# Filter units of four residue classes instead of 128 neighbouring frequencies in a spectral FFN kernel on one Trainium2 core

## The chip, the cores and the metric

The kernel runs on one core of one Trainium2 chip. The metric is device microseconds of one execution; each time is the median of several executions. The engines are PE (matrix multiplies; PEld is its weight load), DVE (vector), ACT (scalar and activation), POOL and SP; POOL and SP also issue DMAs.

## The reference

```python
def _A_ref(x, w_r, w_i):                      # x [1, 2048, 1024], w [2048, 513]
    X = jnp.fft.rfft2(x, axes=(-2, -1))
    X = X * (w_r + 1j * w_i)
    return jnp.fft.irfft2(X, s=(2048, 1024), axes=(-2, -1))
def _B_ref(x, w1, w2):                        # w1 [1024, 3584], w2 [3584, 1024]
    return jnp.einsum("bsf,fd->bsd", _silu(jnp.einsum("bsd,df->bsf", x, w1)), w2)
xn = _layernorm(x)
return x + _A_ref(xn, w_r, w_i) * _silu(_B_ref(xn, w1, w2))
```

All inputs are float32. Two chains start from the layer norm: a feed-forward net (two large products) and a filter in the frequency domain. They meet in the last line.

## The kernel before, in words

**Products.** Each float32 factor is split into two float16 halves (high on ACT, low on DVE), and a product is three float16 matmuls of 128x512. The first product, `mm1`, makes 112 tiles `pa` (4 column groups c of the sequence by 28 feature blocks f) of 24 matmuls each. A tile lies in one of four PSUM buffers (tag `ff`) until ACT takes it out with a SiLU (L441). Four such tiles become `h32`, whose halves `hosum` and `hoone` (L228, L231) are stored by seven DMAs (L464). The second product, `mm2`, is written as seven products m = 0 to 6 of half size over eight row tiles j: 56 tiles `pb` of 42 matmuls each (L510 to L512). The weights of each m are split in 14 steps; a step waits for its raw block `jr`, loaded by POOL (L388).

**The filter.** It runs beside the products, in stages that share PE, DVE and ACT with them:

- Forward: `fa_mat` (L742) transforms rows; ACT takes the result out of PSUM into `L0` (L751, L752), after a DVE memset of one column (L750). `fd_gen` does butterflies on DVE into the tile `V`, then a step R of radix 4 per frequency group j; the halves `Rs` (ACT, L819) are stored to `vd[j]` (POOL, L823).
- `wmax_gen`: the largest filter weight, needed for scaling; 18 loads of 128x912 by SP and 18 reductions on DVE (L859), without stores.
- `f_gen`: 16 filter units u = 4q + j, each 128 rows of the sequence frequency (residue q) by the 128 neighbouring row frequencies of group j. A unit loads `vq` and weights `wq`, runs the matmuls `fx` (L912 to L914) into one of two PSUM buffers (tag `ft`), copies half of it (`xc`, ACT, L935), makes X (DVE), scales the weights by `zs` (ACT, L994), multiplies, makes Z (DVE), and splits Z into halves `zq` (`high_z` on ACT, L952; `low_z` on DVE, L957). Each split is five pieces, since `zq` is ordered by residue class of the row frequency (modulo 16) while a unit holds neighbours. `zq` has one buffer per q; four DMAs (L962) store it when the fourth unit of q is done.
- `edge_gen`: the last frequency column, from `xsv`, 32 small loads by POOL (L1027).
- `i_gen`, for c in the order 1, 3, 0, 2: loads `zt` from `zd[c]` (L1119), runs `iu` (L1146) in four pieces; each is copied by ACT (`uw`, L1153), worked on by DVE, split again (`us`, ACT, L1175); then matmuls `id` (L1188), a copy `sw` (L1195) and butterflies on DVE.

**What sets the order.** Every engine works through its list in order. The lists are written by one Python loop over the `pa` tiles and then the `pb` tiles. After each tile, `work()` takes a step from `wq` (weights), three times in four a step from `xq` (the maxima, the edge), and as many steps from `bg` (the FFT stages) as a cost model of PE and DVE finds room for: a `clock` to which `meter` adds a cost for each instruction as it is written. So fewer or cheaper DVE instructions bring later steps forward in all lists. `defer(n, ...)` issues a store n ticks later; `stores[0]` is SP at first and POOL from the end of the layer norm.

```python
            clock["dve"] = max(clock["dve"], clock["pe"] - 1.0)
            for _ in range(3):
                if clock["dve"] > clock["pe"] + LEAD or hold[0] or slot(bg) == PAUSE:
                    break
```

Tile pools hand out buffers by tag; an instruction that writes a buffer waits for whoever still reads what was in it, stores included.

Of the kernel before, what the change touches and what calls it, by code (L numbers as in the profile page):

```python
# [44 lines left out]
def make_constants():  # L45
# [8 lines left out]
    ca[:, :, 64] = np.where(d0[:, :, 0] % 2 == 0, 1.0, -1.0)  # L54
    ca = np.stack(_halves(ca, 2.0**14), 1)
# [49 lines left out]
def spectral_ffn(ctx, tc, x, w_r, w_i, w1, w2, ca, kc, ci, tw, pm, out):  # L105
# [20 lines left out]
    zd = [dp.tile([128, 4, 2, 1024], F16, name=f"zd{c}") for c in range(4)]  # L126
# [16 lines left out]
    turn2 = cp.tile([128, 128], F32, name="turn2")  # L143
# [459 lines left out]
    A = {}  # L603
# [143 lines left out]
    def fa_evac(c, p):  # L747
        ps = psa.pop((c, p))
        t0 = A["p"].tile([128, 8, 2, 65], F32, name=f"L0_{c}_{p}", tag="L0", bufs=2)
        nc.vector.memset(t0[:, :, 1, 0:1], 0.0)  # L750
        nc.scalar.activation(t0[:, :, 0], ps[:, :, 0:65], AF.Copy)  # L751
        nc.scalar.activation(t0[:, :, 1, 1:64], ps[:, :, 65:128], AF.Copy)  # L752
        l0[c, p] = t0

    def fd_gen(c):
        ap = A["p"]
        vt = ap.tile([128, 4, 2, 512], F32, name=f"V{c}", tag="V", bufs=1)

        def bfly(p):
# [4 lines left out]
            e = ap.tile([128, 4, 2, 65], F32, name=f"E{c}_{p}", tag="E", bufs=1)  # L764
# [3 lines left out]
            ee = ap.tile([128, 2, 2, 65], F32, name=f"EE{c}_{p}", tag="EE", bufs=1)  # L768
            eo = ap.tile([128, 2, 2, 65], F32, name=f"EO{c}_{p}", tag="EO", bufs=1)
# [4 lines left out]
            pq = ap.tile([128, 2, 4, 65], F32, name=f"PQ{c}_{p}", tag="PQ", bufs=1)  # L774
# [16 lines left out]
            tt(v[:, :, 0:65], ee[:, 0], ee[:, 1], op=OP.add)
# [12 lines left out]
            tt(v[:, 1, 0:1], ee[:, 0, 0, 0:1], ee[:, 1, 0, 0:1], op=OP.subtract)  # L804
# [20 lines left out]
        for j in range(4):  # L825
            sl = slice(128 * j, 128 * j + 128)
            if j:
                high_r(j - 1)
# [19 lines left out]
    def wmax_gen():  # L848

        ap = A["p"]  # L850
        mt = small("mw", 18)
        tl = {}
        for k in range(21):
            if k < 18:
                src = (w_r, w_i)[k % 2].rearrange("(p r) k -> p (r k)", p=128)
                tl[k] = ap.tile([128, 912], F32, name=f"wm{k}", tag="x", bufs=4)
                nc.sync.dma_start(tl[k], src[:, 912 * (k // 2):912 * (k // 2) + 912])
            if k >= 3:
                nc.vector.tensor_reduce(mt[:, k - 3:k - 2], tl.pop(k - 3), axis=AX.X, op=OP.max, apply_absolute_value=True)  # L859
# [21 lines left out]
    def f_gen():  # L881
# [36 lines left out]
        for n, t_ in enumerate((ones, ident, turn2)):  # L918
            nc.gpsimd.dma_start(t_, pm[:, n])
# [17 lines left out]
        def by_class(u):  # L937

            j = u % 4
            zv = zs_[u].rearrange("m n (i l) -> m n l i", l=16)  # L940
            qv = [zqs[u // 4][:, k].rearrange("m (n l) i -> m n l i", l=16)[:, :, :, 8 * j:8 * j + 8] for k in range(2)]
            for first, n, to, by in ((1, 3, 0, 4), (4, 4, 14, -4), (9, 4, 3, 4), (13, 3, 9, -4)):
                stop = to + by * (n - 1) + (1 if by > 0 else -1)
                yield zv[:, :, first:first + n], [v[:, :, to:stop if stop >= 0 else None:by] for v in qv]
            yield zv[:, :, 0:9:8], [v[:, :, 12:14] for v in qv]

        def high_z(u):
            q, j = u // 4, u % 4
            if j == 0:
                zqs[q] = bp.tile([128, 2, 128, 32], F16, name=f"zq{q}", tag="zq", bufs=1)  # L950
            for z, o in by_class(u):
                nc.scalar.activation(o[0], z, AF.Copy)  # L952

        def low_z(u):
            q, j = u // 4, u % 4
            for z, o in by_class(u):
                nc.vector.tensor_tensor(o[1], z, o[0], op=OP.subtract)  # L957
# [10 lines left out]
        for u in range(16):  # L968
# [24 lines left out]
            for w in (wr, wi):  # L993
                nc.scalar.activation(w, w, AF.Copy, scale=zs)  # L994
# [34 lines left out]
    def edge_gen():  # L1029
# [267 lines left out]
    with tc.manual_schedule():  # L1297
# [79 lines left out]
        for n, (c, f) in enumerate(order):  # L1377
# [20 lines left out]
            if 44 <= n < 76:  # L1398
                load_edge(n - 44)
# [107 lines left out]
```

## Time and profile before

| what | value |
|---|---|
| median of 3 executions | 1247.46 us (1245.87 to 1251.45) |
| the profiled execution's own time | 1247.57 us |
| its span in the trace | 1245.8 us |
| DMA moved | 296.88 MB, mean 238 GB/s |
| HBM read, written | 186.97 MB, 104.33 MB |

The span runs from the first to the last instruction in the trace. Busy shares are means over stages with different limits, so a change in a stage is judged by that stage's own rows. In a row of a group, "x" is the count; behind the first bar stand the busy time and the mean in ns of one; behind the second the idle time of the engine just ahead of these instructions and what ended it. In a row of the timeline the first number is the start and the second the duration, and the brackets hold the idle time ahead and its releaser.

### The profile page before, as it was taken

To read this page: it belongs to the slowest core of one execution; us is meant where nothing else is said; L and a number is where in the kernel's file an instruction comes from. 1 tells how busy PE (TensorE), PEld (TensorE's weight loads), DVE (VectorE), ACT (ScalarE), POOL (GpSimd) and SP (SyncE) were. 2 spreads that over 40 slices of the span, in tenths; PEclk is the share of its full clock that TensorE was granted. 3 is DMA by queue.
4 is the path that set the end of the run, shared out by engine and by line. 5 is a ranking of instruction groups with operands and counts; after the bars stand their busy time and mean duration, and the time that the engine had idled before them with its cause. 6 is when DMAs were issued, how large, how long until landed. Compare 5 with 4: busy or idle time off the path is not lost. (4 is left out here: it accounts for less than half of the span.)

```text
span 1245.8 us, 20664 instructions
## 1 busy us (share of the span) xinstructions
PE 1225.4 (98%) x7759; PEld 621.0 (50%) x7759; DVE 1018.9 (82%) x2056; ACT 499.4 (40%) x672; POOL 321.1 (26%) x526
## 2 busy tenths in 40 slices
PE   8999999999999999999999999999999998999997
PEld 5545454445455444445545555554555544545544
DVE  6678999998988998565958799894895886895985
ACT  4765354344256356443534335232222222322211
POOL 1341231232444545342333021204123030010000
PEclk9999999999999999999999999999999999999999
DMA  7477475665577789766887889959779699696688
GB/s 239 124 184 192 126 247 171 192 189 159 156 237 229 236 282 332 254 228 180 196 274 229 264 250 245 295 146 360 234 216 301 207 322 375 248 330 240 231 297 317
DMA packets 161733, 296.88 MB, mean 238 GB/s; under 512 B 32048, under 2 KB 84912, under 8 KB 161120
## 3 DMA queue, kind: packets, MB, share of 16 engines
q1 hardware_dynamic: 125392, 183.49, 47.8%
q0 software_dynamic: 36096, 111.93, 28.6%
q8 instruction: 61, 1.00, 0.3%
q14 instruction: 40, 0.33, 0.1%
q10 hardware_dynamic: 144, 0.13, 0.0%
HBM read 186.97 MB, written 104.33 MB: 234 GB/s over the span
## 5 line engine op out<-in xcount | busy, mean ns | idle before, releaser
L432 PE MATMUL pa<-xnT,w 128*128 128x512 f16 x2688 | 585.1, 379 | 2.6 <-DVE xnT L686 1.7
L432 PEld LDWEIGHTS <-w 128*128 128x128 f16 x2688 | 262.3, 98 | 313.4 <-issue 2.0
L510 PE MATMUL pb<-w,ht 128*128 128x512 f16 (+1 forms) x798 | 300.3, 376 | 0.4 <-DMA ht<-hd_one 0.4
L511 PE MATMUL pb<-w,ht 128*128 128x512 f16 (+1 forms) x798 | 300.0, 376 | 0.0
L512 PE MATMUL pb<-w,ht 128*128 128x512 f16 (+1 forms) x798 | 300.0, 376 | 0.0
L512 PEld LDWEIGHTS <-ht 128*128 128x128 f16 x798 | 78.2, 98 | 91.5 <-issue 0.8
L510 PEld LDWEIGHTS <-ht 128*128 128x128 f16 x798 | 78.3, 98 | 90.3 <-issue 0.8
L511 PEld LDWEIGHTS <-ht 128*128 128x128 f16 x798 | 78.3, 98 | 87.2 <-issue 0.6
L441 ACT ACTIVATE h<-pa,s 128x512 f32<-128x512 f32 x112 | 75.2, 677 | 76.7 <-PE pa L432 70.0
L231 DVE SCALAR_TENSOR_TENSOR w<-jr,sc,w 128x512 f16<-128x512 f32 x98 | 71.9, 745 | 33.9 <-ACT w L228 33.8
L228 ACT ACTIVATE w<-jr,sc 128x512 f16<-128x512 f32 x98 | 68.6, 714 | 76.7 <-DMA jr<-in_B_w_dram 69.6
L388 POOL DMA_DIRECT2D jr<-in_B_w_dram x56 | 36.7, 655 | 226.0 <-issue 162.1
L464 POOL DMA_DIRECT2D hd_sum<-hosum x52 | 38.2, 771 | 183.1 <-DVE hosum L231 116.7
L228 ACT ACTIVATE hosum<-hr,hs 128x1536 f16<-128x1536 f32 x28 | 44.0, 1573 | 88.7 <-DVE hr L471 48.0
L952 ACT ACTIVATE zq<-Z 128x192 f16<-128x192 f32 (+2 forms) x80 | 37.2, 542 | 104.0 <-DVE Z L218 67.4
L228 ACT ACTIVATE hoone<-h,hs 128x2048 f16<-128x2048 f32 x28 | 56.0, 1998 | 53.3 <-DMA hd_one<-hoone 22.7
L231 DVE SCALAR_TENSOR_TENSOR hoone<-h,hs,hoone 128x2048 f16<-128x2048 f32 x28 | 65.6, 2343 | 12.0 <-ACT hoone L228 12.0
L470 DVE TENSOR_TENSOR hr<-h 128x1024 f32<-128x1024 f32 x28 | 34.2, 1220 | 35.3 <-ACT h L441 35.1
L464 POOL DMA_DIRECT2D hd_one<-hoone x52 | 46.0, 884 | 66.1 <-DVE hoone L231 21.1
L231 DVE SCALAR_TENSOR_TENSOR hosum<-hr,hs,hosum 128x1536 f16<-128x1536 f32 x28 | 50.7, 1811 | 3.2 <-ACT hosum L228 3.2
L228 ACT ACTIVATE w<-w1r,rs 128x1024 f16<-128x1024 f32 x28 | 31.8, 1143 | 47.6 <-DVE w L231 26.4
L591 ACT ACTIVATE pl<-pl,c 128x512 f32<-128x512 f32 (+1 forms) x26 | 17.0, 683 | 74.7 <-DVE pl L570 45.6
(215 smaller groups left out, 1798.4 us busy)
## 6 DMA issues: line engine op xcount, KB each, us to landing
jr<-in_B_w_dram POOLq DMA_DIRECT2D x84, 256.0 KB, 7.3
w1r<-in_B_w_dram SPq DMA_DIRECT2D x28, 512.0 KB, 5.9
w2m<-in_B_w_dram SPq DMA_DIRECT2D x28, 512.0 KB, 6.3
ht<-hd_dif SPq DMA_DIRECT2D x32, 448.0 KB, 9.5
ht<-hd_sum SPq DMA_DIRECT2D x32, 448.0 KB, 6.2
ht<-hd_one SPq DMA_DIRECT2D x32, 448.0 KB, 7.0
hd_sum<-hosum POOLq DMA_DIRECT2D x52, 256.0 KB, 4.5
hd_one<-hoone POOLq DMA_DIRECT2D x52, 256.0 KB, 4.5
```

Of the source, the lines that this page charges most:

```text
L228: nc.scalar.activation(hi, raw, AF.Copy, scale=scale)
L231: nc.vector.scalar_tensor_tensor(lo, raw, scale, hi, op0=OP.mult, op1=OP.subtract)
L388: nc.gpsimd.dma_start(raw[n], ws[m][q] if m in ws else w2_block(m, q, 0))
L432: nc.tensor.matmul(ps, w[:, wh, d], xt[:, xh, d], start=(n == 0), stop=(n == 23))
L441: nc.scalar.activation(hq[:, 2 * (c % 2) + f % 2], ps, AF.Silu, scale=s1[:, f:f + 1])
L464: defer(1, lambda k=k, m=m: stores[0].dma_start(hd[m, g][:, :, q].rearrange("f p h s -> f p (h s)"), o[:, k].rearrange("f p h s -> f p (h ...
L470: tt(sums[:, 0:2], hq[:, 0::2], hq[:, 1::2], op=OP.subtract)
L510: nc.tensor.matmul(ps, hh[:, 0], w[:, 0], start=first, stop=False)
L511: nc.tensor.matmul(ps, hh[:, 0], w[:, 1], start=False, stop=False)
L512: nc.tensor.matmul(ps, hh[:, 1], w[:, 0], start=False, stop=last)
L591: nc.scalar.activation(o, o, AF.Silu, scale=c2)
L952: nc.scalar.activation(o[0], z, AF.Copy)
```

## The change

The columns of the forward matrix `ca` are put in another order, so that the 128 frequencies of a filter unit are four residue classes of 32 instead of 128 neighbours.

- `fd_gen`: `V` becomes [128, 4, 2, 17, 32], and butterflies write runs of four elements; rows are 68 wide instead of 65, filled by two memsets on POOL instead of one on DVE; two ACT copies per c are new; R goes through j = 3, 2, 1, 0, and for j > 0 its sums and differences take two instructions instead of one (14 instead of 8 per c).
- `wmax_gen`: 16 steps of two loads of 128x512; the last column's maximum comes from `xsv`, in a new job `wmax_end`. Each step also copies its tile in the new column order by five ACT copies into `wc`, which shares the four buffers of tag `x` with the loads, and stores `wc` by two DMAs of 256 KB to the new DRAM tiles `wp`: 80 ACT copies and 32 stores.
- `f_gen` reads the weights from `wp`. The scaling of `wq` goes; `zs` is applied in the splits of Z, which are one instruction per unit (two for j = 0). `zq` is a buffer of its own per unit, two in turn. `zd` is one DRAM tile; each unit stores 512 KB in runs of 256 bytes, where a store before had runs of 2 KB. Three constants are loaded at u = 4 instead of ahead of the stage.
- `load_i` has two DMAs; the loads of `xsv` stand 20 tiles earlier.

```diff
     ca[:, :, 64] = np.where(d0[:, :, 0] % 2 == 0, 1.0, -1.0)
+    col = np.arange(64)
+    kk = 16 * (col % 4) + col // 4
+    ca = ca[:, :, np.concatenate([kk, 64 + kk])]
...
-    zd = [dp.tile([128, 4, 2, 1024], F16, name=f"zd{c}") for c in range(4)]
+    zd = dp.tile([128, 4, 16, 4, 128], F16, name="zd")
+    wp = [dp.tile([S, 512], F32, name=f"wp{i}") for i in range(2)]
...
-        t0 = A["p"].tile([128, 8, 2, 65], F32, name=f"L0_{c}_{p}", tag="L0", bufs=2)
-        nc.vector.memset(t0[:, :, 1, 0:1], 0.0)
-        nc.scalar.activation(t0[:, :, 0], ps[:, :, 0:65], AF.Copy)
+        t0 = A["p"].tile([128, 8, 2, 68], F32, name=f"L0_{c}_{p}", tag="L0", bufs=2)
+        nc.gpsimd.memset(t0[:, :, 1, 0:1], 0.0)
+        nc.gpsimd.memset(t0[:, :, :, 65:68], 0.0)
+        nc.scalar.activation(t0[:, :, 0, 0:65], ps[:, :, 0:65], AF.Copy)
...
-        for j in range(4):
-            sl = slice(128 * j, 128 * j + 128)
...
-            nc.vector.tensor_tensor(b, vt[:, 0:2, :, sl], vt[:, 2:4, :, sl], op=OP.add)
-            nc.vector.tensor_tensor(d, vt[:, 0:2, :, sl], vt[:, 2:4, :, sl], op=OP.subtract)
...
+        for j in (3, 2, 1, 0):
+            parts = ((0, 12, 4),) if j == 0 else ((4 - j, 12 + j, 8 + 2 * j), (4 + j, 12 - j, 8 - 2 * j))
...
+            for o_, op in ((b, OP.add), (d, OP.subtract)):
+                ov = o_.rearrange("a p r (n l i) -> a n (p r) l i", n=len(parts), i=32)
+                for n, (la, lz, st) in enumerate(parts):
+                    nc.vector.tensor_tensor(ov[:, n], *(rows_[:, k:k + 4, la:lz + 1:st] for k in (0, 4)), op=op)
...
-                tl[k] = ap.tile([128, 912], F32, name=f"wm{k}", tag="x", bufs=4)
-                nc.sync.dma_start(tl[k], src[:, 912 * (k // 2):912 * (k // 2) + 912])
...
+                tl[k] = ap.tile([128, 2, 512], F32, name=f"wm{k}", tag="x", bufs=4)
+                for i in range(2):
+                    nc.sync.dma_start(tl[k][:, i], (w_r, w_i)[i][128 * k:128 * k + 128, 0:512])
+            if k >= 2:
+                t_, o = tl.pop(k - 2), ap.tile([128, 2, 512], F32, name=f"wc{k}", tag="x", bufs=4)
+                nc.vector.tensor_reduce(mt[:, k - 2:k - 1], t_, axis=AX.XY, op=OP.max, apply_absolute_value=True)
...
+                nc.scalar.activation(o.rearrange("m r (l i) -> m r l i", i=32)[:, :, 0:4], src[:, :, 0:13:4], AF.Copy)
+                for n, (la, st) in enumerate(((3, -1), (13, 1), (5, 1), (11, -1))):
+                    nc.scalar.activation(dst[:, :, n, 1:4], src[:, :, la:la + 3 * st:st], AF.Copy)
+                for i in range(2):
+                    defer(1, lambda o=o, i=i, k=k: stores[0].dma_start(wp[i][128 * k - 256:128 * k - 128, :], o[:, i]))
...
-            if j == 0:
-                zqs[q] = bp.tile([128, 2, 128, 32], F16, name=f"zq{q}", tag="zq", bufs=1)
+            zqs[u] = bp.tile([128, 2, 8, 128], F16, name=f"zq{u}", tag="zq", bufs=2)
             for z, o in by_class(u):
-                nc.scalar.activation(o[0], z, AF.Copy)
+                nc.scalar.activation(o[0], z, AF.Copy, scale=zs)
...
-            for w in (wr, wi):
-                nc.scalar.activation(w, w, AF.Copy, scale=zs)
...
-            if j == 3:
-                zv = zqs[q].rearrange("m h (c n) i -> m h c (n i)", c=4)
-                for c in range(4):
-                    defer(1, lambda c=c: stores[0].dma_start(zd[c][:, q], zv[:, :, c]))
+            defer(1, lambda: stores[0].dma_start(
+                zd[:, q, :, 3 - j], t_.rearrange("m h n k -> m (h n) k")))
...
-            if 44 <= n < 76:
-                load_edge(n - 44)
+            if 24 <= n < 56:
+                load_edge(n - 24)
```

What this does to the order shows at three places. In these rows the first entry is the line (in the changed kernel lines stand a few later), then the operation, what it writes and reads with a running number behind each name, and the size.

First ACT in the forward stage, between the `pa` tiles of f = 6 and 7. `hosum`, `hoone` and `w1` are the splits of the hidden values and weights. Before:

```order
L751 ACTIVATE L0_1_0_1935<-fa1_0_1885 128x8x65 [waits PE_49]
L752 ACTIVATE L0_1_0_1935<-fa1_0_1885 128x8x63
L441 ACTIVATE h32_3_0_1785<-pa1_7_1850,s1_224 128x512
L228 ACTIVATE w1_9_1970<-w1r9_1567,rs1_223 128x1024 [waits DMAHW2_49,DVE_49,Activation_49]
L751 ACTIVATE L0_1_1_2000<-fa1_1_1910 128x8x65 [waits PE_49]
L752 ACTIVATE L0_1_1_2000<-fa1_1_1910 128x8x63
L228 ACTIVATE hosum_0_3_0_2043<-hr3_0_1965,hs_226 128x12x128 [waits DMASW7_49,DMASW1_49,DMASW0_49]
L441 ACTIVATE h32_3_1_2046<-pa2_6_1939,s1_224 128x512 [waits PE_49]
```

and now:

```order
L445 ACTIVATE h32_3_0_1799<-pa1_7_1880,s1_222 128x512 [waits PE_49]
L232 ACTIVATE w1_9_1950<-w1r9_1570,rs1_221 128x1024 [waits DMAHW2_49,DVE_49,Activation_49]
L877 ACTIVATE wc4_1955<-wm2_1801 128x2x128 [waits DMAHW1_49,DMAHW2_49,DMASW1_49,DMASW0_49]
L879 ACTIVATE wc4_1955<-wm2_1801 128x2x3x32 x4
L756 ACTIVATE L0_1_0_2013<-fa1_0_1963 128x8x65 [waits PE_49,Pool_49]
L757 ACTIVATE L0_1_0_2013<-fa1_0_1963 128x8x63
L232 ACTIVATE hosum_0_3_0_2044<-hr3_0_1945,hs_224 128x12x128 [waits DMASW6_49,DMASW5_49,DMASW4_49]
L445 ACTIVATE h32_3_1_2047<-pa2_6_1919,s1_222 128x512
L877 ACTIVATE wc5_2057<-wm3_1857 128x2x128 [waits DMAHW3_49,DMASW3_49,DMAHW4_49,DMASW2_49,Activation_49]
L879 ACTIVATE wc5_2057<-wm3_1857 128x2x3x32 x4
L756 ACTIVATE L0_1_1_2089<-fa1_1_1988 128x8x65 [waits PE_49,Pool_49]
L757 ACTIVATE L0_1_1_2089<-fa1_1_1988 128x8x63
```

The copies `wc` are new between the evacuations; they wait for DMAs of SP (DMAHW, their loads) and of POOL (DMASW, the stores of the copy one step earlier, whose buffer they write). The evacuation of `L0` waits for POOL as well.

Second ACT in the filter stage, around unit 8. Before:

```order
L935 ACTIVATE xc9_7193<-fx9_7099 128x512 [waits DVE_49,PE_49,Activation_49]
L952 ACTIVATE zq2_7202<-Z8_7195 128x8x3x8 [waits DMASW5_49,DMASW6_49,DMASW0_49,DMASW7_49,DVE_49,Activation_49]
L952 ACTIVATE zq2_7202<-Z8_7195 128x8x4x8
L952 ACTIVATE zq2_7202<-Z8_7195 128x32x8
L952 ACTIVATE zq2_7202<-Z8_7195 128x8x3x8
L952 ACTIVATE zq2_7202<-Z8_7195 128x8x2x8
```

and now:

```order
L960 ACTIVATE xc9_7197<-fx9_7120 128x512 [waits DVE_49,PE_49,Activation_49]
L971 ACTIVATE zq8_7206<-Z8_7199,zs_216 128x8x64 [waits DMASW4_49,DVE_49]
L971 ACTIVATE zq8_7206<-Z8_7199,zs_216 128x8x64
...
L960 ACTIVATE xc10_7323<-fx10_7245 128x512 [waits DVE_49,PE_49,Activation_49]
L971 ACTIVATE zq9_7332<-Z9_7325,zs_216 128x1024 [waits DMASW6_49,DVE_49]
```

Four stores were waited for at the first unit of each q; now each unit waits for the one store of the unit two before it.

Third ACT in the inverse stage, around the first piece of c = 0. `w2_5` are the weight splits for m = 5 of the second product, `pl4_j` the SiLU behind its tiles of m = 4. Before:

```order
L591 ACTIVATE pl4_2_1_10521<-pl4_2_1_10521,c2_228 128x512
L228 ACTIVATE w2_5_1_10488<-jr82_10527,sc2_229 128x512
L228 ACTIVATE w2_5_1_10488<-jr83_10559,sc2_229 128x512
L591 ACTIVATE pl4_3_1_10599<-pl4_3_1_10599,c2_228 128x512
L1153 ACTIVATE uw0_0_10806<-iu0_0_10708 128x512
L1175 ACTIVATE us0_0_10907<-uu0_0_10818 128x1024
L1153 ACTIVATE uw0_1_10910<-iu0_1_10757 128x512
```

and now:

```order
L595 ACTIVATE pl4_1_1_10494<-pl4_1_1_10494,c2_226 128x512
L232 ACTIVATE w2_5_1_10539<-jr79_10498,sc2_227 128x512
L1175 ACTIVATE uw0_0_10712<-iu0_0_10614 128x512
L232 ACTIVATE w2_5_1_10539<-jr80_10531,sc2_227 128x512
L232 ACTIVATE w2_5_1_10539<-jr81_10536,sc2_227 128x512
L1197 ACTIVATE us0_0_10823<-uu0_0_10724 128x1024
L1175 ACTIVATE uw0_1_10826<-iu0_1_10663 128x512
L595 ACTIVATE pl4_2_1_10572<-pl4_2_1_10572,c2_226 128x512
L232 ACTIVATE w2_5_1_10539<-jr82_10577,sc2_227 128x512
```

`uw0_0` stood behind `pl4_3` and all splits for m = 5; now it stands two tiles earlier, and four of these splits come behind it, between the pieces of c = 0.

More of the change, by code (lines that the diff above doesn't have):

```diff
@@ L756, in fd_gen @@
         ap = A["p"]
-        vt = ap.tile([128, 4, 2, 512], F32, name=f"V{c}", tag="V", bufs=1)
+        vt = ap.tile([128, 4, 2, 17, 32], F32, name=f"V{c}", tag="V", bufs=1)
         def bfly(p):
@@ L763, in bfly @@
             tt(t0[:, :, 0, 64], t0[:, :, 0, 64], A["tw"][:, 0:8], op=OP.mult)
-            e = ap.tile([128, 4, 2, 65], F32, name=f"E{c}_{p}", tag="E", bufs=1)
+            e = ap.tile([128, 4, 2, 68], F32, name=f"E{c}_{p}", tag="E", bufs=1)
             o = t0[:, 4:8]
@@ L767, in bfly @@
             tt(o, t0[:, 0:4], t0[:, 4:8], op=OP.subtract)
-            ee = ap.tile([128, 2, 2, 65], F32, name=f"EE{c}_{p}", tag="EE", bufs=1)
-            eo = ap.tile([128, 2, 2, 65], F32, name=f"EO{c}_{p}", tag="EO", bufs=1)
+            ee = ap.tile([128, 2, 2, 68], F32, name=f"EE{c}_{p}", tag="EE", bufs=1)
+            eo = ap.tile([128, 2, 2, 68], F32, name=f"EO{c}_{p}", tag="EO", bufs=1)
             tt(ee, e[:, 0:2], e[:, 2:4], op=OP.add)
@@ L773, in bfly @@
             tt(t0[:, 1], o[:, 1], o[:, 3], op=OP.add)
-            pq = ap.tile([128, 2, 4, 65], F32, name=f"PQ{c}_{p}", tag="PQ", bufs=1)
+            pq = ap.tile([128, 2, 4, 68], F32, name=f"PQ{c}_{p}", tag="PQ", bufs=1)
             pp, qq = pq[:, 0], pq[:, 1]
@@ L837, in fd_gen @@
             o[j] = r.rearrange("a (q r) k -> a q (r k)", r=2)
+            last = j
             yield 3.9
-        high_r(3)
+        high_r(0)
         yield 0.5
-        low_r(3)
+        low_r(0)
         yield 1
@@ L917, in f_gen @@
         load_k(0)
-        for n, t_ in enumerate((ones, ident, turn2)):
-            nc.gpsimd.dma_start(t_, pm[:, n])
         yield PAUSE
@@ L937, in by_class @@
         def by_class(u):
[L939 to L945, printed above, removed]
+            src, dst = zs_[u].rearrange("m n (l i) -> m n l i", l=4), zqs[u].rearrange("m h n (l i) -> m h n l i", l=4)
+            for to, n, at in ((0, 4, 0),) if u % 4 else ((0, 2, 0), (2, 2, 1)):
+                yield src[:, :, at:4:4 // n], [dst[:, h, :, to:to + n] for h in range(2)]
         def high_z(u):
-            q, j = u // 4, u % 4
-            if j == 0:
-                zqs[q] = bp.tile([128, 2, 128, 32], F16, name=f"zq{q}", tag="zq", bufs=1)
+            zqs[u] = bp.tile([128, 2, 8, 128], F16, name=f"zq{u}", tag="zq", bufs=2)
             for z, o in by_class(u):
-                nc.scalar.activation(o[0], z, AF.Copy)
+                nc.scalar.activation(o[0], z, AF.Copy, scale=zs)
         def low_z(u):
@@ L984, in f_gen @@
                 nc.gpsimd.tensor_copy(xsv[:, 0, q], Xv[:, :, :, 0])
+            if u == 4:
+                assert w1j.done
+                B["turn2"] = turn2 = bp.tile([128, 128], F32, name="turn2")
+                for n, t_ in enumerate((ones, ident, turn2)):
+                    nc.gpsimd.dma_start(t_, pm[:, n])
             if u == 13:
@@ L1053, in edge_gen @@
             nc.tensor.matmul(ps[:, n * 32:n * 32 + 8], ident, rv[:, n, 0].rearrange("m a r -> m (a r)"), start=True, stop=False)
-            nc.tensor.matmul(ps[:, n * 32:n * 32 + 8], turn2, r0[:, n].rearrange("m a r -> m (a r)"), start=False, stop=True)
+            nc.tensor.matmul(ps[:, n * 32:n * 32 + 8], B["turn2"], r0[:, n].rearrange("m a r -> m (a r)"), start=False, stop=True)
         yield 1
@@ L1118, in load_i @@
         zt = C["p"].tile([128, 4, 2, 2, 16, 32], F16, name=f"zt{c}", tag="zt", bufs=1)
-        nc.sync.dma_start(zt.rearrange("m q h r l i -> m q h (r l i)"), zd[c])
+        for h in range(2):
+            nc.sync.dma_start(zt[:, :, h].rearrange("m q r l i -> m q (r l i)"), zd[:, :, 8 * h + 2 * c:8 * h + 2 * c + 2].rearrange("m q r g k -> m q (r g k)"))
         k = C["p"].tile([128, 4, 2, 3, 64], F16, name=f"kk{c}", tag="kk", bufs=1)
@@ L1384, in spectral_ffn @@
                 add(xq, wmax_gen())
-                max_job = add(xq, w2max_gen())
+                add(xq, w2max_gen())
+                max_job = add(xq, wmax_end())
                 f_job = add(bg, switch(A, open_f, 1, max_job))
```

56 lines of the change are left out of this document (32 added, 24 removed).

## The prediction

> **What bounds the kernel now.** I read the busy times first, then what the matrix engine (PE) waits for, then the stages.
>
> ```profile
> span 1245.8 us, 20664 instructions
> ...
> PE 1225.4 (98%) x7759; PEld 621.0 (50%) x7759; DVE 1018.9 (82%) x2056; ACT 499.4 (40%) x672; POOL 321.1 (26%) x526
> ```
>
> PE is idle for 20.4 us of 1245.8, and the change leaves every matmul in place. So the work itself gives nothing; a gain can only come out of those 20.4 us, and a loss only out of new ones. The list of what PE waits for says where they are:
>
> ```profile
> PE iu L1146 <- DVE uw L1157: 3.5, 2, 2.4
> PE fx L912 <- ACT xc L935: 1.9, 1, 1.9
> ...
> PE pa L432 <- DVE xnT L686: 1.7, 1, 1.7
> ...
> PE pb L510 <- DMA ht<-hd_one: 0.4, 1, 0.4
> ```
>
> Columns: total us, times, longest. `xnT` belongs to the start. In the middle stand three: 3.5 (inverse stage), 1.9 (filter stage) and 0.4 (a load), 5.8 together. The stages show the rest:
>
> ```profile
> 100.00:200.00 100.00, 99.78 (x573) 49.83 (x571) 94.52 (x211) 45.27 (x51) 25.84 (x35) 1.00 0.64 185
> 750.00:800.00 50.00, 48.07 (x319) 26.91 (x317) 49.06 (x91) 20.41 (x38) 11.83 (x27) 1.00 0.99 264
> 1000.00:1050.00 50.00, 48.54 (x349) 23.78 (x348) 35.19 (x81) 12.09 (x19) 13.73 (x20) 1.00 1.06 345
> 1230.00:1245.80 15.80, 8.32 (x77) 7.22 (x74) 8.06 (x17) 3.17 (x6) 0.00 (x0) 0.90 0.75 258
> ```
>
> After the window come its length, the busy time of PE, weight loads, DVE, ACT and POOL, the granted clock, and the share of the DMA engines. The tail holds 15.80 - 8.32 = 7.5 idle us, and 20.4 - 7.5 - 5.8 = 7.1 are left for the start; the change touches neither. During the forward transform (100 to 200) PE is full, DVE nearly so, ACT has half of its time left. In the filter stage DVE has nothing left. In the inverse stage the DMA engines have nothing left.
>
> A stall costs more than its length when the clock falls behind it:
>
> ```profile
> 1045.23 1.51 PE L1146 MATMUL iu<-kk,zt 64*128 64x128 f16 x48 [1.05 <-DVE uw L1157]
> 1046.67 0.39 PE L510 MATMUL pb<-w,ht 128*128 128x512 f16 x1
> ...
> 1053.81 1.78 PE L1146 MATMUL iu<-kk,zt 64*128 64x128 f16 x48 [2.43 <-DVE uw L1157]
> 1055.52 0.61 PE L510 MATMUL pb<-w,ht 128*128 128x512 f16 x1
> 1055.92 0.63 PE L511 MATMUL pb<-w,ht 128*128 128x512 f16 x1
> ...
> 1058.40 0.38 PE L511 MATMUL pb<-w,ht 128*128 128x512 f16 x1
> ```
>
> Behind the gap of 1.05 the 48 small matmuls take 1.44 us from start to start (1046.67 - 1045.23); behind the one of 2.43 they take 1.71, and the next seven large ones 2.88 (1055.52 to 1058.40) instead of 7 x 0.22 = 1.54. So the 2.43 us stall cost 0.27 + 1.34 = 1.6 more. Everything that could be won is 5.8 + 1.6 = 7.4 us, 0.6%. The Trainium skill ("TensorE: Matmul & The Clock Gate", What's actually happening) has the clock fall to half only after at least one idle window of about 3.4 us; by that the stall would have cost 2.43 alone and the total would be 5.8. The rows show the fall behind 2.43 us, and they decide.
>
> **The change part by part.** *Filter units.* The five pieces per unit of the high and low halves of Z become one (two in every fourth unit), and the two scalings of the weights go:
>
> ```profile
> L952 ACT ACTIVATE zq<-Z 128x192 f16<-128x192 f32 (+2 forms) x80 | 37.2, 542 | 104.0 <-DVE Z L218 67.4
> L994 ACT ACTIVATE wq<-wq,zs 128x512 f32<-128x512 f32 x32 | 21.2, 710 | 0.0
> L957 DVE TENSOR_TENSOR zq<-Z,zq 128x192 f16<-128x192 f32 (+2 forms) x80 | 34.5, 494 | 5.6 <-ACT zq L952 5.5
> L228 ACT ACTIVATE w<-w1r,rs 128x1024 f16<-128x1024 f32 x28 | 31.8, 1143 | 47.6 <-DVE w L231 26.4 <-DVE rs L259 14.7 <-issue 6.4
> L231 DVE SCALAR_TENSOR_TENSOR w<-w1r,rs,w 128x1024 f16<-128x1024 f32 x28 | 35.7, 1276 | 5.5 <-ACT w L228 5.5
> L228 ACT ACTIVATE w<-jr,sc 128x512 f16<-128x512 f32 x98 | 68.6, 714 | 76.7 <-DMA jr<-in_B_w_dram 69.6 <-DMA jr<-ws 6.0 <-PE pb L512 1.1
> L231 DVE SCALAR_TENSOR_TENSOR w<-jr,sc,w 128x512 f16<-128x512 f32 x98 | 71.9, 745 | 33.9 <-ACT w L228 33.8
> ```
>
> ACT loses 80 x 0.542 + 32 x 0.710 = 66.1 us and gets 12 x 1.143 + 8 x 0.714 = 19.4 (the split of the weights is the same operation at both sizes): 47 less. DVE loses 80 x 0.494 = 39.5 and gets 12 x 1.276 + 8 x 0.745 = 21.3: 18 less, 1.1 per unit, where it had nothing left. The second thing that goes is a wait:
>
> ```profile
> 747.33 2.29 ACT L952 ACTIVATE zq<-Z 128x192 f16<-128x192 f32 x5 [9.72 <-DMA zd<-zq]
> ...
> 759.19 2.33 ACT L952 ACTIVATE zq<-Z 128x192 f16<-128x192 f32 x5 [4.74 <-DVE Z L218]
> ...
> 767.15 0.72 ACT L228 ACTIVATE w<-jr,sc 128x512 f16<-128x512 f32 x1 [3.18 <-DMA jr<-ws]
> 767.78 0.58 ACT L935 ACTIVATE xc<-fx 128x512 f32<-128x512 f32 x1
> ```
>
> The first unit of a new group rewrites the one buffer `zq` and waits until its four stores have landed (9.72 us). The copy `xc` at 767.78, for which PE then stood 1.9 us, came late through that and through a late load right ahead of it. With `zq` in two buffers per unit and a lighter DVE I take the 1.9 as gone (bounds: 0 to -1.9, the load may be as late again).
>
> *Inverse stage.* Of the change only the halves of the `zt` load touch it, but since the filter work is cheaper and starts earlier in the order, the inverse pieces move up by about two tiles of `pb` (42 large matmuls each, 42 x 0.22 = 9.2 us). The 3.5 + 1.6 us arose where `uw` for c = 0 was queued on ACT behind work that waited for loads:
>
> ```profile
> 1019.93 0.72 ACT L228 ACTIVATE w<-jr,sc 128x512 f16<-128x512 f32 x1 [2.90 <-DMA jr<-in_B_w_dram]
> ...
> 1027.13 0.72 ACT L228 ACTIVATE w<-jr,sc 128x512 f16<-128x512 f32 x1 [2.45 <-DMA jr<-in_B_w_dram]
> ...
> 1042.64 0.72 ACT L591 ACTIVATE pl<-pl,c 128x512 f32<-128x512 f32 x1 [5.18 <-DMA fx<-in_A_x_dram]
> 1043.27 0.58 ACT L1153 ACTIVATE uw<-iu 128x512 f32<-128x512 f32 x1
> ```
>
> Behind the change the last splits of `jr` stand between the `uw` pieces instead of ahead of all of them. One such split waits 2.5 to 2.9 us and takes 0.72; the `pl` step waited 5.18. Bounds: -5.1 if the new neighbours are on time; +5 if two more gaps like the 2.43 one appear (2 x 4.0 = 8, less what the old place cost, some 3). Between such ends I take -2.5, half of the gain, since each single new wait is shorter than the 5.18 that made the old stall.
>
> *Forward stage.* DVE gets 24 more adds of R in pieces (14 instead of 8 per column group c) and rows of 68 instead of 65; it loses 16 memsets. Adding pieces costs their fixed part: of the 494 ns mean of short pieces above not more than half, 24 x 0.25 = 6 us, over some 300 us of which DVE has 5.5 idle in each 100. PE does not wait for it there; I cost it at nothing as long as the idle 5.5% covers it. The maximum reads 16 x 1024 instead of 18 x 912 values per partition, the same work.
>
> ACT gets what the filter stage lost: 5 copies in each of 16 steps, 80 x 0.542 = 43.4 us, and POOL 32 stores of 256 KB. What counts is the wait: step k's copies write the buffer that was freed by step k-1's stores, and ACT, in order, stands until they have landed. Queued behind that on ACT are the evacuations of `pa` (four PSUM buffers), for which PE waits in the end.
>
> ```profile
> L432 PE MATMUL pa<-xnT,w 128*128 128x512 f16 x2688 | 585.1, 379 | 2.6 <-DVE xnT L686 1.7
> ...
> L441 ACT ACTIVATE h<-pa,s 128x512 f32<-128x512 f32 x112 | 75.2, 677 | 76.7 <-PE pa L432 70.0
> ...
> L352 POOL DMA_DIRECT2D ws<-wd x42 | 25.8, 651 | 62.7 <-DVE wd L351 53.1 <-DVE V L791 6.3 <-DVE L L763 2.6
> L464 POOL DMA_DIRECT2D hd_one<-hoone x52 | 46.0, 884 | 66.1 <-DVE hoone L231 21.1
> ...
> 144.44 1.57 ACT L228 ACTIVATE hosum<-hr,hs 128x1536 f16<-128x1536 f32 x1 [7.47 <-DMA hd_sum_d<-hosum]
> ...
> hd_one<-hoone POOLq DMA_DIRECT2D x52, 256.0 KB, 4.5
> ...
> ws<-wd POOLq DMA_DIRECT2D x42, 256.0 KB, 5.7
> ...
> zd<-zq POOLq DMA_DIRECT2D x16, 512.0 KB, 8.5
> ```
>
> A tile of `pa` is 585.1/112 = 5.2 us of PE, so PE stops when ACT is more than three tiles, 15.7 us, late. A step takes 5 x 0.542 + 2 x 0.651 + 5.7 = 9.7 us from its first copy to the landing. Where steps lie one tile apart, ACT falls 4.5 us behind; where two, it catches up 0.7. The order has two places (steps 3 to 7 and 10 to 14) with two short spacings each, so ACT is late by 9 us at the worst, on top of what it was late before: between 0.7 (just the evacuation) and the 9.0 us of the row at 144 us (7.47 + 1.57), which PE did not notice. The sum is 9.7 to 18, against 15.7: nothing, or a stall of some 2.3 us at each place. Where four `hd` stores stand ahead on POOL (4 x 0.884 = 3.5) it is 3.5 worse. The Pool memsets ahead of the `L` evacuation sit in that same queue. Bounds 0 to 2 x 5.8 = 12; I take +2, near the row that PE did not notice.
>
> *The store of Z* has runs of 256 bytes instead of 2 KB. The rows of `hd_one` (512-byte runs, 4.5 us) and `ws` (2 KB runs, 5.7) show no price of short runs down to 512; 256 is outside them. I take 0, and a rival below holds the other end. `xsv` loads 20 tiles earlier and the late `ident` loads: nothing waits for them.
>
> Sum against the profiled execution's own 1247.57 (median of three 1247.46, the same): -1.9 - 2.5 + 2.0 = -2.4, so **1245.2**.
>
> **The rivals.** *All stalls go* (1240.2): 1247.6 - 7.4. For: the 47 us off ACT and 18 off DVE lie in the stages where they arise. Against: the inverse stalls came from loads, at a DMA share of 1.06, and that stays. 0.12.
>
> *ACT stands behind its own stores in the forward stage* (about 1256): slower. Place: 130 to 300 us, deciding once ACT is 15.7 us late. Price: 5.8 us at two places, and 1.6 of slow clock behind each, 14.8, less 4.4 of gain and about 2 that fall together: +8.4. For: the wait is certain, and three sorts of store share POOL. Against: ACT is 45% busy there, and a 9.0 us hold cost nothing. 0.18.
>
> *The inverse pieces meet late weights* (about 1253): the splits of `jr` now between `uw` pieces of c = 0, and of c = 3 likewise, make two stalls of 2.9 with 1.6 of clock more than before, 9, less 1.9 and some 1.5: +5.5. 0.10.
>
> *The 256-byte runs are slow* (about 1280). Two units (747.33 to 773.27 on ACT, 26 us) pass until a buffer is rewritten, and its store is issued about one unit after the first half was written, so 13 us are left; 8.5 + 0.7 fit. At twice the landing time, 17, ACT is 4.7 us late in each unit, of which slack eats half: 14 x 2.4 = 33. The Trainium skill ("DMA: Bandwidth & Descriptors", Specifications) says that transfers under 512 B fall below line rate and are read, modified and written; a doubling would be what this rival has. No row of the trace goes below 512 bytes on a store. 0.04.
>
> *Nothing changes* (1247.6): the copy `xc` stays late through the `jr` load, inverse stalls as before. 0.06.
>
> **How the numbers follow.** The forecast has 0.50 (1242 to 1250), the rivals 0.12, 0.18, 0.10, 0.04, 0.06. A measurement of this kernel tells about 0.5%, 6.2 us, from no change: faster means under 1241.2, slower over 1253.7. Faster is the first rival, 0.12. Slower is nearly all of the second, half of the third, all of the fourth, 0.25; the rest, 0.63, is the same. The range begins at 1240, the sum with every stall gone, and ends at 1259, the second rival with its places some 3 us dearer; beyond are the slow stores and the tail of the second, about 0.1, and below 0.05.
>
> **What would show it.** Right: no wait of ACT `zq` for `zd`; `fx` gone from PE's waits; the `iu` wait smaller; PE full from 100 to 300 us; ACT showing waits `wc` for `wp` of up to 7 us. Wrong: PE waits `pa` for ACT `h` between 130 and 300 us (second rival); `iu` waits above 3.5 us with `jr` as what ACT waits for (third); `zd` landing in 15 us or more (fourth). A time under 1241 would mean that the inverse stalls depended on the filter stage, over 1254 that a queue behind a store reached PE.

## The result and the profile after

The changed kernel took 1254.07 us (median of 7, 1253.11 to 1257.32), the one before 1245.87 (7, 1244.53 to 1251.45): ratio 1.0062, 95% interval [1.0044, 1.0081]. It is slower by 8.2 us where 2.4 us less was forecast. Its profiled execution took 1253.11 us with a span of 1251.3, 5.5 longer than the one before; the rest of the 8.2 is that the two profiled executions lie 1.7 above and 1.0 below their medians.

What PE waits for in the changed kernel (columns: total us, times, longest):

```profile
PE iu L1168 <- DVE uw L1179: 5.1, 2, 3.7
PE pa L436 <- DVE w L235: 4.3, 1, 4.3
...
PE pa L436 <- ACT h L445: 1.9, 1, 1.9
```

and the stages in which this lies (after the window: its length; busy PE, weight loads, DVE, ACT and POOL; the granted clock, the DMA share and GB/s):

```profile
150.00:200.00 50.00, 45.66 (x259) 22.42 (x258) 42.07 (x62) 27.65 (x37) 21.34 (x36) 0.97 0.72 224
250.00:300.00 50.00, 48.08 (x263) 23.55 (x261) 43.91 (x70) 34.28 (x56) 25.82 (x41) 1.00 0.82 263
750.00:800.00 50.00, 50.00 (x329) 27.91 (x327) 44.16 (x76) 11.03 (x16) 17.12 (x25) 1.00 0.87 257
1000.00:1050.00 50.00, 44.92 (x368) 23.22 (x366) 31.51 (x63) 12.50 (x19) 15.34 (x22) 0.97 1.05 330
```

The filter stage is as forecast: PE is full from 750 to 800 us, where it had lacked 1.9, `fx` is gone from the list, and DVE, which had been busy 49.06 of these 50 us, is busy 44.16. The forward stage, where PE had been full, now has two stalls of 4.3 and 1.9 us. The inverse stage stalls as before or more.

**First stall, at 162 us.** The changed kernel's ACT, DVE and PE:

```profile
153.43 2.00 ACT L232 ACTIVATE hoone<-h,hs 128x2048 f16<-128x2048 f32 x1 [5.80 <-DMA hd_one<-hoone]
...
156.95 1.04 ACT L827 ACTIVATE Rs<-Ro 128x1024 f16<-128x1024 f32 x1
...
158.02 1.23 DVE L830 SCALAR_TENSOR_TENSOR Rs<-Ro,Rs 128x1024 f16<-128x1024 f32 x1 [5.82 <-ACT Rs L827]
...
160.63 1.27 DVE L235 SCALAR_TENSOR_TENSOR w<-w1r,rs,w 128x1024 f16<-128x1024 f32 x1
...
161.97 16.83 PE L436 MATMUL pa<-xnT,w 128*128 128x512 f16 x70 [4.26 <-DVE w L235]
```

The same work in the kernel before:

```profile
146.64 1.05 ACT L819 ACTIVATE Rs<-Ro 128x1024 f16<-128x1024 f32 x1
152.45 2.00 ACT L228 ACTIVATE hoone<-h,hs 128x2048 f16<-128x2048 f32 x1 [4.76 <-DMA hd_one<-hoone]
...
156.10 1.28 DVE L231 SCALAR_TENSOR_TENSOR w<-w1r,rs,w 128x1024 f16<-128x1024 f32 x1 [2.43 <-ACT w L228]
...
157.44 15.28 PE L432 MATMUL pa<-xnT,w 128*128 128x512 f16 x70 [0.22 <-DVE w L231]
```

Before, the evacuation `Rs` stood on ACT ahead of the split `hoone`, which waits some 5 us for its stores. Now it stands behind it. DVE waits for `Rs` (5.82 us), then makes the next `Ro`, and only then the low half of the weights `w1`, which PE needs. In both kernels this low half is made at the last moment (0.22 us of stall before); 4.5 us later it is late by 4.3, and the slow clock behind the gap adds 1.5. Of the 4.5 us, 1.0 is that `hoone` itself is released later (153.43 instead of 152.45), and 3.5 are what DVE now does for R ahead of the low half. No weight copy had run by then; the first starts at 170 us.

**Second stall, at 259 us.** PE and ACT:

```profile
256.78 0.28 PE L239 MATMUL s<-m,ones 128*128 128x2 f32 x2
258.98 1.24 PE L436 MATMUL pa<-xnT,w 128*128 128x512 f16 x5 [1.92 <-ACT h L445]
```

```profile
248.20 1.99 ACT L232 ACTIVATE hoone<-h,hs 128x2048 f16<-128x2048 f32 x1
250.09 0.67 ACT L445 ACTIVATE h<-pa,s 128x512 f32<-128x512 f32 x1
256.07 0.63 ACT L877 ACTIVATE wc<-wm 128x256 f32<-128x256 f32 x1 [5.31 <-DMA wp<-wc]
256.61 1.75 ACT L879 ACTIVATE wc<-wm 128x192 f32<-128x192 f32 x4
258.26 0.67 ACT L445 ACTIVATE h<-pa,s 128x512 f32<-128x512 f32 x1
```

A weight copy waits 5.31 us for the store of the copy before it, and the evacuation of `pa` stands behind it.

**Inverse stage.** ACT and PE:

```profile
1030.99 0.58 ACT L1175 ACTIVATE uw<-iu 128x512 f32<-128x512 f32 x1
1033.73 0.72 ACT L232 ACTIVATE w<-jr,sc 128x512 f16<-128x512 f32 x1 [2.16 <-DMA jr<-in_B_w_dram]
1036.68 0.72 ACT L232 ACTIVATE w<-jr,sc 128x512 f16<-128x512 f32 x1 [2.23 <-DMA jr<-in_B_w_dram]
1037.31 1.04 ACT L1197 ACTIVATE us<-uu 128x1024 f16<-128x1024 f32 x1
1038.26 0.57 ACT L1175 ACTIVATE uw<-iu 128x512 f32<-128x512 f32 x1
```

```profile
1032.95 1.51 PE L1168 MATMUL iu<-kk,zt 64*128 64x128 f16 x48 [1.34 <-DVE uw L1179]
1042.85 2.74 PE L1168 MATMUL iu<-kk,zt 64*128 64x128 f16 x48 [3.75 <-DVE uw L1179]
```

Two weight splits, each late by its load, stand between the first and the second `uw`: the third rival's place. The stalls are 1.34 and 3.75, and the piece behind the second takes 2.74 instead of 1.51: 6.3 us, where it had been 1.05 + 2.43 + 1.6 = 5.1.

In sum: 5.6 at the first place (4.26 + 1.5, less the 0.22 that stood there before), 1.9 at the second and 1.2 at the third, and 0.5 by which PE was already later ahead of the first stall; less 1.9 (`fx`) and 0.4 (`ht`), less 1.4 because the tail behind the last matmul is shorter (6.1 instead of 7.5). That is the 5.5 us by which the spans differ.

### The profile page after: what moved, and what is told of

Same layout as the page of the kernel before. It is cut to its first block, busy times and chain, and to the rows that moved or that the text cites. A ratio compares the mean times of both kernels' runs of the same rounds, so it can differ in the third digit from the quotient of the medians.

```text
span 1251.3 us, 20737 instructions
## 1 busy us (share of the span) xinstructions
PE 1225.6 (98%) x7759; PEld 621.3 (50%) x7759; DVE 1008.9 (81%) x2003; ACT 499.0 (40%) x668; POOL 357.9 (29%) x590
## 4 chain that ended last, share of the span: by engine, by line
PE 72%; DVE 3%; DMA 2%; issue 1%; POOL 1%; ACT 0%; SPq 0%; DVEq 0%; POOLq 0%; ACTq 0%
PE pa L436 29%; PE pb L514 12%; PE pb L516 12%; PE pb L515 12%; PE fx L939 2%; PE iu L1168 2%; PE id L1210 1%; PE fx L941 1%; PE fx L940 1%; DMA jr<-in_B_w_dram 1%; DMA fx<-in_A_x_dram 0%; DMA out_dram<-pl 0%; POOL jr L396 0%; PE fa L746 0%; PE fa L747 0%
## 5 line engine op out<-in xcount | busy, mean ns | idle before, releaser
L939 PE MATMUL fx<-vq,kq 128*128 128x256 f16 x192 | 43.2, 272 | 0.0
```

What stands on the lines that cost most here:

```text
L939: nc.tensor.matmul(o, k[:, c, kh, 1], v[:, c, vh], start=(n == 0), stop=False)
```

## The experiments

Theory A: the change loses in three separate places, each by where a waiting instruction stands in an engine's order. Against it stand B (the added stores and copies slow the forward stage as a whole), D (late loads, whatever the order), and others named below. Ratios are to the kernel before on the same chip. One execution of each run was traced, so a trace need not lie at the median.

**No copies, no stores.**

```diff
-                t_, o = tl.pop(k - 2), ap.tile([128, 2, 512], F32, name=f"wc{k}", tag="x", bufs=4)
+                t_ = tl.pop(k - 2)
...
-                nc.scalar.activation(o.rearrange("m r (l i) -> m r l i", i=32)[:, :, 0:4], src[:, :, 0:13:4], AF.Copy)
-                for n, (la, st) in enumerate(((3, -1), (13, 1), (5, 1), (11, -1))):
-                    nc.scalar.activation(dst[:, :, n, 1:4], src[:, :, la:la + 3 * st:st], AF.Copy)
-                for i in range(2):
-                    defer(1, lambda o=o, i=i, k=k: stores[0].dma_start(wp[i][128 * k - 256:128 * k - 128, :], o[:, i]))
...
-                    nc.sync.dma_start(t_[64 * b:64 * b + 64], wpv[i][q][b, :, :, 128 * j:128 * j + 128])
+                    nc.sync.dma_start(t_[64 * b:64 * b + 64], wv[i][q][b, :, :, 128 * j:128 * j + 128])
```

> The changed kernel without the five copies of each weight tile into the new column order and without the two stores behind them; the filter units read the weights in their old order, so the filter is not the reference's. Theory A (three separate places: 5.9 us at 162 us from a shift in the order of ACT and DVE, 2.1 us at 259 us from a copy that waits for its store, 5.2 us in the inverse stage): only the 1.9 us stall in front of pa at 259 goes, the 4.3 us stall at about 162 stays: about 1252. Theory B (the traffic and the queue of the new stores make the forward stage late as a whole): both forward stalls go: about 1246. Theory C (the copies cost nothing): no change, 1254.

1253.26 us, 1.0046 [1.0033, 1.0059]. The stall at 259 us is gone, the one on `w1` stays (4.0 us at 161). B falls for the first stall.

**The clock charges step R as before.** Same instructions; only the cost clock that sets the order is told that R is two full-width instructions. By its formula a step in four pieces costs 4 x (0.07 + 256 x 0.001045) = 1.35 us instead of 1.21, so 0.14 us for each such step is all that the edit takes out.

```diff
+            mark = clock["dve"]
             for o_, op in ((b, OP.add), (d, OP.subtract)):
...
+            clock["dve"] = mark + 2 * (0.07 + 512 * 1.045e-3) * pace[0]
```

> The changed kernel with the same instructions, but the cost clock charges step R as before the change (two full-width instructions instead of four half ones); in the order of ACT the first R evacuation then stands ahead of the wait for the stores of hoone again. Theory A: the 4.3 us stall on the low half of w1 at about 162 us goes, with its half clock: 1254 - 5.9 = about 1248; the stall at 259 and those in the inverse stage stay unless later steps move too. Theory B (the added DVE work itself or the new stores are the cost, wherever they stand): stays at 1254.

1253.45 us, 1.0049 [1.0031, 1.0066]. The first stall is gone, with no DVE work taken away. But the time is the same, as B had said, since the second stall has grown (the traced execution is the longest of its six, 1256.42 us). PE, then ACT:

```profile
PE pa L436 <- DVE w L235: 0.3, 1, 0.3
...
259.78 33.80 PE L436 MATMUL pa<-xnT,w 128*128 128x512 f16 x144 [6.76 <-ACT h L445]
```

```profile
242.38 0.64 ACT L879 ACTIVATE wc<-wm 128x256 f32<-128x256 f32 x1 [9.59 <-DMA wp<-wc]
...
256.87 0.63 ACT L879 ACTIVATE wc<-wm 128x256 f32<-128x256 f32 x1 [5.49 <-DMA wp<-wc]
```

ACT's waits of copies for stores, first in the changed kernel, then here:

```profile
ACT wc L877 <- DMA wp<-wc: 16.6, 4, 5.3
ACT wc L877 <- issue: 9.5, 2, 6.2
```

```profile
ACT wc L879 <- DMA wp<-wc: 33.1, 8, 9.6
```

The two lists do not compare like with like: in the changed kernel another 9.5 us of such waits stand under "issue", with no releaser seen. The rows show it better. The copy that holds ACT up starts at 256.07 in the changed kernel and at 256.87 here, nearly the same; but PE, which isn't stopped at 162 us here, is out of work at 253.02 (259.78 - 6.76) instead of 257.06 (258.98 - 1.92). So the 4 us won at the first place are lost again at the second: 6.8 us of stall with 2.5 of slow clock. My expectation took the places as independent; it was too low by 5 us in the median, and by 7 in this trace's second stall with its clock.

**The shift alone, in the kernel before.**

```diff
+            if c == 0 and j == 1:
+                yield PAUSE
             if j:
                 high_r(j - 1)
```

> The kernel before with one edit: the second step R of column group 0 is put off by one slot, nothing else is added. Theory A: the same stall on the low half of w1 appears at about 160 us, 3 to 4.5 us and about 1.5 of half clock: slower by 4 to 6, about 1251. Theory B: the place in the order does not matter, 1246.

1251.24 us, 1.0035 [1.0025, 1.0046], 4.7 us slower than the 1246.51 beside it. One slot of delay, and nothing added, makes the first stall: `Rs` stands behind `hoone` here too.

```profile
152.49 2.00 ACT L228 ACTIVATE hoone<-h,hs 128x2048 f16<-128x2048 f32 x1 [5.79 <-DMA hd_one<-hoone]
...
156.00 1.04 ACT L819 ACTIVATE Rs<-Ro 128x1024 f16<-128x1024 f32 x1
```

```profile
161.02 14.16 PE L432 MATMUL pa<-xnT,w 128*128 128x512 f16 x57 [3.85 <-DVE w L231]
```

**The copies alone, in the kernel before.** `wmax_gen` is replaced by the changed one; nothing reads `wp`.

> The kernel before with the changed maximum alone: 16 steps of two loads, the five copies and two stores of each weight tile, which nobody reads then (the last frequency column is left out of the maximum). Theory A: ACT is not held up at 162 us, so the waits for the stores reach PE as in the run with the clock's charge: a stall of 5 to 9 us near 260 us, about 1252 to 1255. Theory B' (the copies only hurt together with the new forward stage): no stall, 1246.

1255.69 us, 1.0068 [1.0039, 1.0096]: 9.4 slower, as much as the whole change, though the five executions spread from 1250.11 to 1257.88. PE's waits in the longest but one (1257.66):

```profile
PE pa L433 <- ACT h L442: 3.0, 3, 1.7
PE fa L743 <- ACT L L753: 2.7, 1, 2.7
```

The size is about as expected, the shape is not: several stalls of 0.5 to 2.7 us between 250 and 550 us, `fa` among them, instead of one. Not all of the 9.4 belongs to them: the `iu` waits are 2.0 us longer in this trace as well.

**Neither the shift nor the copies.** The edits of the first two runs together.

> The changed kernel with the clock's charge for step R as before, and without the copies and stores of the weights (the filter units read them in the old order, so the filter is not the reference's). Theory A: both forward stalls are gone, what is left is the filter's gain of 2 us and the inverse stage's 5 us as before: about 1244 to 1246. Theory E (one of the two stalls always appears, since ACT or DVE is at its limit in the forward stage): a stall of 3 us or more somewhere from 150 to 300 us, about 1250.

1245.46 us, 0.9990 [0.9976, 1.0005]. No forward stall is left. The four runs make a table:

| the changed kernel | copies and stores | without |
|---|---|---|
| clock as changed | 1254.07 | 1253.26 |
| clock charges R as before | 1253.45 | 1245.46 |

The four were not all timed on one chip, so the ratios to the kernel before are the better measure: against 0.9990, each cause alone costs 0.0056 and 0.0059, some 7 us, and both together 0.0072, 9 us, where independent causes would cost 14. Each ratio is uncertain by 1.5 to 2.5 us. That is why taking one away gained so little.

**Two buffers for the copies.** The clock as before, and the tiles are copied one step after their load instead of two, so that of the four buffers two are left for the copies.

```diff
-        for k in range(18):
+        for k in range(17):
...
-            if k >= 2:
-                t_, o = tl.pop(k - 2), ap.tile([128, 2, 512], F32, name=f"wc{k}", tag="x", bufs=4)
+            if k >= 1:
+                t_, o = tl.pop(k - 1), ap.tile([128, 2, 512], F32, name=f"wc{k}", tag="x", bufs=4)
```

> The changed kernel with the clock's charge for step R as in the run before and, beside it, the weight tiles copied one step after their load instead of two, so that two of the four buffers are left for the copies and a copy waits for the stores two steps back. Theory A (the copies cost through the wait for their own last store): no PE stall on ACT's h between 150 and 300 us, 9.4 us less than with the clock's charge alone: about 1244 to 1246. Theory B (the traffic of the stores and the copies' own 40 us of ACT are the cost): a stall of 5 us or more stays near 260 us, about 1252.

1246.17 us, 0.9999 [0.9988, 1.0010]. All copies and stores are there, and the wait is gone from PE's list; what ACT still waits for stores:

```profile
ACT wc L879 <- DMA wp<-wc: 6.3, 2, 5.5
```

So it is the wait for the last store that costs, not the traffic or the 40 us of copies on ACT (0.7 us above the run without them on the same chip, within the intervals). B falls for the second stall too: added DVE work, copies and stores are all there, and the time is that of the kernel before. The edit also brings each copy one step forward in the order; what that does by itself wasn't tried.

**The inverse of c = 0 later.** By two tiles in the changed kernel (3 slots more):

```diff
-        for _ in range(1 if c == IORDER[0] else 3):
+        for _ in range({1: 1, 0: 6}.get(c, 3)):
```

> The changed kernel with the inverse of column group 0 started some two tiles later, so that all weight splits of the sixth product stand ahead of its pieces on ACT. Theory A (the pieces wait behind splits whose loads are late): the two iu stalls (1.3 and 3.7 us, 5.2 with the clock) go or shrink to under 1.5: about 1249 to 1250. Theory D (the DMA engines are full there, so whatever stands in the queue is late): stalls of 3 to 5 us stay, 1253 to 1255.

1257.22 us, 1.0080 [1.0051, 1.0109]: no gain (the changed kernel had 1.0062, and the intervals overlap). The splits stand ahead of all pieces, as wanted, but a `pl` step behind `uw` now waits for its load on DVE, and PE behind it:

```profile
1047.81 0.69 DVE L562 TENSOR_TENSOR pl<-pl,pb 128x512 f32<-128x512 f32 x1 [5.36 <-DMA pl<-pd]
```

```profile
1051.01 2.74 PE L1168 MATMUL iu<-kk,zt 64*128 64x128 f16 x48 [5.91 <-DVE uw L1179]
```

This speaks for D: out of the way of one late load, the pieces meet another, and the DMA share there is 1.04 (1000 to 1050 us). Then by four tiles (9 in the place of 6), on top of the two buffers:

> The kernel with two buffers for the copies and the clock's charge, and the inverse of column group 0 started some four tiles later, behind the SiLU of the tiles 3 and 4 of the fifth product. Theory D (loads are late while the DMA engines are full, up to about 1050 us): past that the iu stalls shrink below 1.5 us: 1240 to 1242 if the forward stalls are gone too. Theory A (the pieces stall behind whichever step waits for a load): stalls of 3 to 6 us stay, about 1246.

1244.00 us, 0.9983 [0.9974, 0.9993]: faster than both kernels, by 2.3 us than the kernel before. The `iu` stalls are gone, as D had said, but the time stays 2 us above what D gave: one load `ht` stops PE for 2.65 us instead, which was not expected.

**The later inverse without the change, and both again.**

> The kernel before with one edit: the inverse of column group 0 started later, so that its first piece stands behind the SiLU of tile 4 of the fifth product, as in the run with two buffers and the later inverse. Theory A (the inverse stalls belong to the order there and not to the change): the two iu stalls of before (5.0 us with their half clock) shrink to under 2, 1242 to 1244. Theory F (the gain there came from the changed filter): no change, 1246.

> The kernel with two buffers for the copies, the clock's charge for step R as before and the later inverse once more, beside the run before it on one chip: what the changed filter itself is worth, once the order is mended in both. Theory A: the filter's stall of 2 us is gone here and stays in the other kernel, so about 1 to 2 us less than it, near 1242 to 1244. Theory F: equal to it.

On one chip, beside 1245.95 us of the kernel before: the kernel before with the later inverse takes 1251.09, 1.0048 [1.0030, 1.0065]; the changed one, mended and with the later inverse, 1244.17, 0.9983 [0.9973, 0.9993]. Both theories missed the first; the second is 6.9 us faster than it, where 1 to 2 were expected. In the first the `iu` stalls are gone, and PE ends earlier than in any run before it, but the tail is longer. First its tail, then that of the mended kernel (columns as above):

```profile
1187.00:1235.10 48.10, 47.35 (x425) 27.68 (x423) 43.54 (x107) 9.04 (x15) 0.00 (x0) 1.00 0.88 298
1235.10:1248.90 13.80, 0.00 (x0) 0.00 (x0) 7.60 (x17) 2.72 (x6) 0.00 (x0) 0.66 0.67 227
```

```profile
1187.00:1235.50 48.50, 48.50 (x348) 27.07 (x346) 40.15 (x94) 8.65 (x14) 0.00 (x0) 1.00 0.92 315
1235.50:1243.40 7.90, 0.00 (x0) 0.00 (x0) 4.77 (x12) 0.91 (x2) 0.00 (x0) 0.76 0.51 184
```

Behind the last matmul 13.8 us pass instead of 7.9. The last `id` pieces, first of the kernel before, then with the later inverse, then of the mended kernel:

```profile
1182.21 1.51 PE L1188 MATMUL id<-cis,us 64*128 64x128 f16 x48
```

```profile
1206.14 1.51 PE L1188 MATMUL id<-cis,us 64*128 64x128 f16 x48
```

```profile
1197.51 1.51 PE L1212 MATMUL id<-cis,us 64*128 64x128 f16 x48
```

The later start of c = 0 moves the last inverse, c = 2, and at 1206 us it comes too close to the end: DVE is busy 43.54 of the last 48 us and has 7.60 us of work left when PE is done. In the mended kernel, with c = 0 put off to the same place, the last piece stands at 1197.51. Its gain over the kernel before is 1.8 us, no more than the filter's 1.9 us stall; what the two runs add is that the kernel before loses by this late inverse and the changed one doesn't. Whether another delay would help the kernel before wasn't tried.

## Why the prediction was wrong, point by point

- *The 1.9 us of `fx` go*: right. The splits of Z cost what was estimated (1.143 and 1.276):

```profile
L976 DVE SCALAR_TENSOR_TENSOR zq<-Z,zs,zq 128x1024 f16<-128x1024 f32 x12 | 15.3, 1277 | 1.3 <-ACT zq L971 1.3
L971 ACT ACTIVATE zq<-Z,zs 128x1024 f16<-128x1024 f32 x12 | 13.8, 1146 | 28.7 <-DVE Z L222 28.7
```

- *Step R costs nothing, since DVE's idle 5.5% covers it*: this is the step that failed, and it carries 5.8 us (4.3 of stall and 1.5 of slow clock), put at nothing. The added time on DVE was small, as said: the sums and differences of R keep it busy for 23.4 us instead of 21.8, 1.6 more where 6 were estimated. But the same instructions add 0.14 us per step to the cost clock, and that moved R by one slot, behind a wait of ACT. The run with the old charge and the one with the shift alone show it. I had read the clock's effect in the inverse stage and not in the forward stage, where the change adds DVE work; the two places of ACT's order that I looked at there lay behind 170 us.
- *The waits for the stores of the copies cost +2*: the mechanism was right, and in the profile it had nearly this size (1.9). That size was no bound: with the first stall gone it is 6.8 plus 2.5 of slow clock, and in the kernel before the copies cost 9.4 in all, 2 of them in `iu` waits. The bounds of 0 to 12 held it. The number of free buffers was too high: a matmul `s` for the scales stands ahead of the stalled tile (256.78) and takes one of the four, so that ACT may be two tiles late there and not three. That follows from the row and the tag; it wasn't tried.
- *The inverse stage gives half of its 5.1 back*: wrong, it took 1.2 more, 3.7 us from the forecast. That each new wait is shorter than the old 5.18 did not help, because several follow each other between the pieces. The third rival's place was right, its price too high.
- *The 256-byte stores cost nothing*: right in that nothing waits for them; a store lands in 6.6 us, far from the 15 that would have shown the fourth rival. POOL is busy longer with issuing one, 1228 ns instead of 719:

```profile
vd<-Rs POOLq DMA_DIRECT2D x16, 512.0 KB, 5.4
...
zd<-zq POOLq DMA_DIRECT2D x16, 512.0 KB, 6.6
```

```profile
L979 POOL DMA_DIRECT2D zd<-zq x16 | 19.7, 1228 | 51.1 <-DVE zq L976 46.5 <-issue 2.8 <-DMA jr<-ws 1.8
```

The 8.5 us before do not measure the price of short runs, since those stores were issued four in a row and these one at a time. Beside the stores `vd`, of the same size and in longer runs (5.4 us), they land 1.2 us later. So the rule of the Trainium skill ("DMA: Bandwidth & Descriptors", Specifications) on transfers under 512 bytes is neither borne out nor refuted here; a doubling of the landing time is not seen.

- *The second rival, about 1256, at 0.18*: near the result by its sum, but by luck: in the trace the place that it named cost 1.9 us, and 5.6 came from one that it did not name. That the range held the time is luck for the same reason, since its upper end was this rival's. The sign did not hold: R was put at nothing, and the inverse stage was taken near its good end.

## What to carry to other kernels

Where a cost model sets the order of several engines, dearer work in one stage is a change of order there, even if an engine has room for it (here 0.14 us in the model moved a step by a slot): look for the nearest in-order wait that a step can fall behind, and for the consumer that is already served at the last moment (here 0.22 us of slack). Two stalls in sequence can hide each other, so a cause is cleared only when both are taken away together. A copy that is stored should have a second buffer before it is put on an engine that also evacuates PSUM.

## What was not expected of the hardware

The clock fell behind stalls of 2.43 us (the kernel before), 3.75 and 4.26 (the changed one), 5.91 and 6.76: in the changed kernel some 7 matmuls behind the 4.26 us came about 0.43 us apart instead of 0.22 (1.5 us lost), with the clock's charge some 12 behind the 6.76 (2.5 us). Behind 1.92 us none did. Two runs with the later inverse add stalls of 2.65 and 2.87 us, in front of a load `ht`:

```profile
1037.98 0.61 PE L514 MATMUL pb<-w,ht 128*128 128x512 f16 x1 [2.65 <-DMA ht<-hd_one]
```

```profile
1037.31 0.39 PE L514 MATMUL pb<-w,ht 128*128 128x512 f16 x1 [2.87 <-DMA ht<-hd_one]
```

Behind the 2.65 us the slow matmuls come at once; behind the 2.87, four matmuls run at full rate, and from 1038.57 to 1041.55 they come 0.43 us apart. So the clock falls with a delay that differs, and the first matmul behind a stall need not show it yet. The Trainium skill ("TensorE: Matmul & The Clock Gate", What's actually happening) has half rate behind at least one idle window of about 3.4 us; the longer stalls agree with that, those of 2.43, 2.65 and 2.87 us do not.
